# Sixteen counters in place of twelve for the transfers of a two-layer attention and MLP kernel

## The chip, the cores and the metric

The kernel runs on one core of a Trainium2 chip. A core has five engines with an instruction stream each: PE (matrix products), ACT (activation functions), DVE (elementwise work and reductions), POOL (elementwise work) and SP (which here only issues transfers). Each engine runs its own stream strictly in order; streams meet only through semaphores, which one instruction raises and another waits for. Transfers (DMAs) are issued by SP and, for two of them, by ACT; each raises its semaphore by 16 when it has landed. The metric is the device time of one execution in microseconds (us), and the number to predict is the median of several runs.

## The reference

Two layers, each of sliding-window attention and an MLP, both with a layer norm ahead and a residual behind, on one sequence of 2048 tokens of width 512:

```python
def _A_ref(x, wqkv, wo):                 # H = 32 heads, Dh = 16, window W = 256
    q, k, v = split(x @ wqkv)
    scores = einsum("bhqd,bhkd->bhqk", q, k) * (Dh ** -0.5)
    mask = (i - j >= 0) & (i - j < W)
    p = softmax(where(mask, scores, -1e9))
    return merge_heads(p @ v) @ wo

def _B_ref(x, w1, b1, w2, b2):           # F = 1792
    return gelu(x @ w1 + b1) @ w2 + b2

x = A_x
for _ in range(2):                       # the same weights both times
    x = x + _A_ref(layernorm(x), A_wqkv, A_wo)
    x = x + _B_ref(layernorm(x), B_w1, B_b1, B_w2, B_b2)
```

All inputs are bfloat16. B_x is not used.

## The kernel before

**Tiling.** The 2048 tokens are 16 tiles of 128 rows, held in SBUF as `X` for the whole program; two layers make 32 tile steps. A pair of tiles is an attention block (16 blocks, `attention`, line 894); the MLP takes two to four tiles at a time (`JOBS`, line 361; `mlp`, line 1080). For each tile `layernorm` (line 723) runs a chain: `bn_stats` and `bn_aggr` on DVE (lines 730 and 732), an addition of epsilon (line 734), a power on POOL (`rstd`, line 737), the scaling `xn` on DVE (line 740), and then a transposition, on PE (line 36 in the profile, by way of `_Slots.transpose`) with a copy out of PSUM (`evac`, line 714), or for later tiles through a scratch tensor in HBM by two transfers (`put` and `get`, lines 755 to 763). Projections to Q, K and V follow (`first_proj`, line 827, for the first block; `proj`, line 834), K by a product with a parity mask (lines 850 and 858), then the scores (line 928), the exponential on ACT (`E`, line 937), the mask (line 958), the product with V (line 1010), and the output projection. All matmuls go through `_Slots.matmul`, so the profile shows them as line 32.

**Order.** Each operation is a node. The list `ORDER` (line 413) fixes one global order of all nodes by hand, which fixes each engine's stream; `TURNS` and `BANKS` fix which engine takes an operation that has a choice, and the PSUM banks. `_List.run` (line 231) only works out planned start and end times for that order. Nothing of this depends on the number of counters.

**Waits.** `_Sched.op` (line 89) is called for each node in the global order. It works out what the node must wait for: the last writer of all that it reads, the last writer and the readers of all that it writes. A dictionary `know` holds what each engine is already sure of, from its own earlier waits and, through `snap`, from what the engine it waited for knew; a wait that is already covered is left out. For a transfer there is one wait more: transfers take the counters `dma0`, `dma1`, ... in turn, whoever issues them, and a transfer waits until the transfer before it on its counter has landed (lines 98 to 102):

```python
        if dma:
            counter = "dma%d" % (self.dma_rr % self.N_DMA_SEMS)
            self.dma_rr += 1
            inc = 16
            need(counter, self.cnt_val[counter])
```

`spread` (line 135) takes matmul operations that have more than one wait and puts the further ones at earlier matmuls, if the planned times allow it. `wait_all_dma` (line 131) makes SP wait for every counter at the end.

**The loads at the start.** There are fifteen, emitted in this order: 0 is tile 0 of X; 1 to 4 are quarters of the Q and K parts of Wqkv (Q first half, K first half, Q second half, K second half); 5 the V part; 6 the tiles 4 to 7 of X; 7 b1; 8 Wo; 9 the tiles 8 to 15 of X; 10 W1; 11 W2; 12 b2 (broadcast to 128 rows); all on SP. 13 is tile 1 of X and 14 the tiles 2 and 3, both issued by ACT, where they are the first instructions. The next transfer (15) comes at 114 us and belongs to the MLP's layer norm; in all there are 120, the last 17 of which write the output, mixed with the others.

```python
        load_x(0, 1, 2450.0)
        load_x(1, 1, 2650.0, "act")
        load_x(2, 2, 4500.0, "act")
```

**PE at the start.** `clear` (line 666) runs 13 matmuls on zeros (lines 675 and 676) ahead of all other PE work.

Of the kernel before, what the change touches and what calls it, by code (L numbers as in the profile page):

```python
# [55 lines left out]
class _Sched:  # L56

    ENGINES = ("pe", "act", "dve", "pool", "sp")
    N_DMA_SEMS = 12
    LOOK = 96  # L60
    COUNTERS = ("pe", "act", "dve", "pool") + tuple("dma%d" % i for i in range(N_DMA_SEMS))

# [26 lines left out]
    def op(self, eng, fn, reads=(), writes=(), inc=1, dma=False, start=0.0, end=0.0, n=1, joins=(), behind=None):  # L89
# [8 lines left out]
# [3 lines that stand above are left out]
# [1099 lines left out]
```

## Time and profile before

| | |
|---|---|
| device time, median of 3 runs | 460.27 us (459.19 to 461.04) |
| device time of the profiled execution | 463.4 us |
| its span, first to last instruction | 461.5 us |
| mean granted PE clock | 0.985 |
| PE busy | 438.4 us, 95% |
| ACT busy | 387.4 us, 84% |
| DVE busy | 369.4 us, 80% |
| POOL busy | 239.4 us, 52% |

The profile's page gives busy time by engine, the span in 40 equal slices (a digit is tenths), and the chain of work that ended last: followed back from the last instruction, at each step to what released it. Further views of the trace give that chain in order of time, a timeline of merged instructions (start, length, engine, line, operation, written and read tiles; in brackets the idle time of the engine before it and what ended it), sums by stretch of time with the granted PE clock, and for transfers the time from issue to landing. A letter q behind an engine's name (SPq, ACTq) is its sequencer, which issues transfers and waits. PEld is PE's loading of weights, which overlaps the matmuls.

### The profile page before, as it was taken

How to read it: one execution, taken by the hardware profiler on the slowest of the kernel's cores; microseconds unless marked ns; L12 is line 12 of the kernel's file. 1: busy time of each engine (PE TensorE's matmuls, PEld its weight loads, DVE VectorE, ACT ScalarE, POOL GpSimd, SP SyncE). 2: the span in 40 equal slices, each digit the busy share in tenths (PEclk: the TensorE clock that was granted, in tenths of full speed). 3: DMA queues.
4: the chain of work that ended last, by engine and by line, in shares of the span. 5: the costliest groups of instructions: out<-in, count | busy, mean ns of one | idle time of the engine just before them, and what ended most of it. 6: DMA issues, size and time to landing. Idle time of an engine off the chain costs nothing.

```text
span 461.5 us, 19292 instructions
## 1 busy us (share of the span) xinstructions
PE 438.4 (95%) x8764; PEld 233.9 (51%) x8764; DVE 369.4 (80%) x723; ACT 387.4 (84%) x462; POOL 239.4 (52%) x297
## 2 busy tenths in 40 slices
PE   4898999898998999999999999999999999999997
PEld 1755563554453454554444545445464453445665
DVE  1899988889995799997988789998999877777602
ACT  1399999999996998897998899989988899784262
POOL 2357466662756445663588726575534515291230
PEclk8699999999998999999999999999999999999999
DMA  8920000000150031521031011222312202012101
GB/s 255 371 71 4 5 3 1 4 2 9 40 98 3 13 38 41 98 40 26 24 83 26 13 26 37 72 42 33 59 37 62 37 24 68 7 50 60 57 1 45
DMA packets 74462, 22.87 MB, mean 50 GB/s; under 512 B 61324, under 2 KB 73868, under 8 KB 74380
## 3 DMA queue, kind: packets, MB, share of 16 engines
q1 hardware_dynamic: 73964, 21.24, 19.8%
q8 instruction: 68, 1.11, 1.0%
q10 hardware_dynamic: 416, 0.39, 0.3%
q14 instruction: 14, 0.11, 0.1%
HBM read 13.77 MB, written 7.86 MB: 47 GB/s over the span
## 4 chain that ended last, share of the span: by engine, by line
PE 77%; ACT 14%; DVE 3%; DMA 3%; issue 1%; SPq 0%
PE ps L32 77%; ACT E L937 12%; DMA X<-in_A_x_dram 1%; DMA scr_x<-xs_ 1%; DVE KT L858 1%; DMA Wqkv_sb<-in_A_wqkv_dram 1%; ACT gT L1103 1%; PE ps L36 1%; DVE stat L730 0%; DVE xs_ L750 0%; DVE X L795 0%; ACT gT L1095 0%; ACT L937 0%; ACT L1103 0%; DVE TT L1023 0%
## 5 line engine op out<-in xcount | busy, mean ns | idle before, releaser
L937 ACT ACTIVATE E<-ps 128x1024 bf16<-128x1024 f32 x304 | 285.9, 1045 | 24.1 <-PE ps L32 22.8
L958 POOL TENSOR_TENSOR E<-E,mask 128x512 bf16<-128x512 bf16 (+1 forms) x128 | 134.3, 1063 | 91.8 <-DVE E L958 33.3
L32 PE MATMUL ps<-W_sb,gT 128*128 128x512 bf16 (+1 forms) x462 | 119.8, 374 | 0.9 <-issue 0.6
L32 PE MATMUL ps<-xnTB,W_sb 128*128 128x512 bf16 (+1 forms) x560 | 116.5, 339 | 1.1 <-ACT E L937 0.5
L32 PE MATMUL ps<-xnTA,Wqkv_sb 128*128 128x256 bf16 (+1 forms) x544 | 75.6, 273 | 2.0 <-ACT E L937 1.2
L32 PEld LDWEIGHTS ps<-xnTB,W_sb 128*128 128x128 bf16 x560 | 51.3, 98 | 46.0 <-ACT E L937 5.1
L1103 ACT ACTIVATE gT<-ps,b1T 128x512 bf16<-128x512 f32 (+1 forms) x92 | 48.4, 589 | 25.1 <-PE ps L32 24.7
L795 DVE TENSOR_TENSOR X<-X,ps 128x512 bf16<-128x512 bf16 x63 | 42.6, 678 | 32.3 <-PE ps L32 31.8
L32 PE MATMUL ps<-QT,KT 32*64 32x320 bf16 (+4 forms) x2976 | 65.5, 259 | 2.8 <-ACT E L937 1.2
L32 PEld LDWEIGHTS ps<-W_sb,gT 128*128 128x128 bf16 x462 | 41.0, 98 | 44.5 <-issue 8.1
L32 PEld LDWEIGHTS ps<-xnTA,Wqkv_sb 128*128 128x128 bf16 x544 | 48.9, 101 | 24.5 <-ACT E L937 4.3
L958 DVE TENSOR_TENSOR E<-E,mask 128x512 bf16<-128x512 bf16 (+1 forms) x134 | 52.8, 421 | 3.6 <-ACT E L937 3.3
L32 PEld LDWEIGHTS ps<-QT,KT 32*64 32x64 bf16 x2976 | 27.8, 103 | 49.5 <-ACT E L937 32.5
L32 PE MATMUL ps<-E,Va 64*17 64x128 bf16 (+3 forms) x3872 | 46.5, 229 | 5.5 <-issue 3.0
L730 DVE BATCH_NORM_STATS2 stat<-X 128x6 f32<-128x512 bf16 x64 | 43.2, 680 | 9.5 <-DMA X<-in_A_x_dram 9.1
L1023 DVE STREAM_TRANSPOSE TT<-ps 128x1024 f32<-128x1024 f32 x32 | 39.9, 1247 | 13.1 <-PE ps L32 12.8
L737 POOL TENSOR_TENSOR rstd<-veps,mhalf 128x1 f32<-128x1 f32 x64 | 37.2, 586 | 24.3 <-DVE veps L734 22.5
L32 PEld LDWEIGHTS ps<-E,Va 64*17 64x17 bf16 x3872 | 36.7, 85 | 22.5 <-PE ps L32 8.2
L1028 POOL TENSOR_TENSOR TM<-TT,Rc 128x512 bf16<-128x512 f32 x21 | 22.2, 1058 | 43.9 <-DVE Rc L1026 31.4
L1067 POOL TENSOR_TENSOR X<-X,b2b 128x512 bf16<-128x512 bf16 x32 | 36.7, 1156 | 12.0 <-DVE E L958 6.5
L858 DVE TENSOR_TENSOR KT<-ps,parmask 128x1024 bf16<-128x1024 f32 x30 | 36.3, 1209 | 4.9 <-PE ps L32 4.8
L32 PE MATMUL ps<-Wqkv_sb,xnTA 128*128 128x512 bf16 x128 | 37.6, 386 | 0.4 <-issue 0.3
(52 smaller groups left out, 343.0 us busy)
## 6 DMA issues: line engine op xcount, KB each, us to landing
scr_x<-xs_ SPq DMA_DIRECT2D x44, 128.0 KB, 2.0
W_sb<-in_B_w_dram SPq DMA_DIRECT2D x2, 1792.0 KB, 15.2
xnTB<-scr_x SPq DMA_DIRECT2D x26, 128.0 KB, 2.7
xnTA<-scr_x SPq DMA_DIRECT2D x18, 128.0 KB, 3.7
out_dram<-X SPq DMA_DIRECT2D x15, 128.0 KB, 1.8
Wqkv_sb<-in_A_wqkv_dram SPq DMA_DIRECT2D x4, 256.0 KB, 4.1
X<-in_A_x_dram SPq DMA_DIRECT2D x1, 1024.0 KB, 10.7
Wqkv_sb<-in_A_wqkv_dram SPq DMA_DIRECT2D x1, 512.0 KB, 6.3
```

The source lines that it names most:

```text
L32: return self.e.matmul(*a, **k)
L36: return self.e.transpose(*a, **k)
L730: add("dve", lambda e, B: e.bn_stats(stat6[:, k6, :], X[:, t, :]), 590, reads=["X%d" % t], writes=["st%d" % k6], prio=prio)
L737: add("pool", lambda e, B: e.tensor_tensor(out=rstd[:, k : k + 1], in0=veps[:, k : k + 1], in1=mhalf[:], op=ALU.pow), 535, reads=["ve%d" % ...
L795: add("dve", lambda e, B: e.tensor_tensor(out=X[:, t, :], in0=X[:, t, :], in1=ps[:, B[g][0], :], op=ALU.add), d_psum(512), reads=["X%d" % ...
L858: add("dve", lambda e, B, g=g, i=i: e.tensor_tensor(out=KT[:, kb, :, 2 * i : 2 * i + 2, :].rearrange("p a c q -> p a (c q)"), in0=ps[:, B[ ...
L937: add("act", lambda e, B, g_=g_, gi=gi: e.activation(E[:, 2 * gi : 2 * gi + 2, e0 : e0 + 512], ps[:, B[g_][0] : B[g_][0] + 2, :], AF.Exp, ...
L958: op = lambda e, B, Ew=Ew, Mw=Mw: e.tensor_tensor(out=Ew, in0=Ew, in1=Mw, op=ALU.mult)
L1023: add("dve", lambda e, B: e.transpose(TT[:, s].rearrange("p a c q d -> p a (c q d)"), ps[:, B[g][0] : B[g][0] + 2, :].rearrange("p a n -> ...
L1028: mul = lambda e, B: e.tensor_tensor(out=TM[:, sm].rearrange("p c q a d -> p a (c q) d"), in0=TT[:, s, :, :, :, 0:Dh].rearrange("p a c q d ...
L1067: add("pool", lambda e, B: e.tensor_tensor(out=X[:, t, :], in0=X[:, t, :], in1=b2b[:], op=ALU.add), 1110, reads=["X%d" % t, "b2b"], writes ...
L1103: add("act", lambda e, B, g=g, fc=fc: e.activation(gT[:, fc, 0:M], ps[:, B[g][0], 0:M], AF.Gelu_apprx_tanh, bias=b1T[:, fc : fc + 1], scal ...
```

## The change

The number of counters for transfers goes from 12 to 16. With it the tuple `COUNTERS`, the semaphores taken, the turn in which transfers take them, and the waits at the end follow.

```diff
@@ -56,7 +56,7 @@
 class _Sched:
 
     ENGINES = ("pe", "act", "dve", "pool", "sp")
-    N_DMA_SEMS = 12
+    N_DMA_SEMS = 16
     LOOK = 96
     COUNTERS = ("pe", "act", "dve", "pool") + tuple("dma%d" % i for i in range(N_DMA_SEMS))
```

Transfer number k takes counter k mod 16 in place of k mod 12, and waits for number k - 16 in place of k - 12. Order, engines and PSUM banks stay as they are.

## The prediction

> **What bounds the kernel now.** I read the page's head and its clock row first, then the first stretch of the chain of waits, then the timelines of ACT, DVE and PE there, and last the windows that cover the hand-over to the long middle part.
>
> ```profile
> span 461.5 us, 19292 instructions
> ...
> PEclk8699999999998999999999999999999999999999
> ```
>
> The span is 461.5 us of a profiled execution of 463.4 us, so 1.9 us lie around it. The clock row is lowest in the first two slices (11.5 us each). So the start is unlike the rest, and the chain of waits says why:
>
> ```profile
> 1.22 3.14 DMA Wqkv_sb<-in_A_wqkv_dram
> 4.37 0.02 issue
> 4.39 6.76 DMA X<-in_A_x_dram
> ...
> 13.30 0.61 ACT xnTA L718
> 13.90 0.05 issue
> 13.95 0.61 PE ps L32 x4
> ```
>
> The chain goes from a weight load that lands at 1.22 + 3.14 = 4.36 us straight into the load of an X tile, which waits for no weight. That is a borrowed wait: tile 1 of X (128 rows) needs nothing from Wqkv. The timelines of ACT, DVE, POOL and PE give the rest:
>
> ```profile
> 4.39 1.35 ACTq L689 DMA_DIRECT2D X<-in_A_x_dram  x2
> ```
> ```profile
> 2.84 0.69 DVE L730 BATCH_NORM_STATS2 stat<-X 128x6 f32<-128x512 bf16 x1 [1.66 <-DMA X<-in_A_x_dram]
> 3.57 0.18 DVE L732 BATCH_NORM_AGGREGATE statmv<-stat 128x2 f32<-128x6 f32 x1
> 11.18 0.69 DVE L730 BATCH_NORM_STATS2 stat<-X 128x6 f32<-128x512 bf16 x1 [7.42 <-DMA X<-in_A_x_dram]
> ...
> 12.12 0.15 DVE L734 TENSOR_SCALAR veps<-statmv 128x1 f32<-128x1 f32 x1
> 12.19 0.41 DVE L740 TENSOR_SCALAR xn<-X,statmv,rstd 128x512 bf16<-128x512 bf16 x1
> ...
> 18.01 0.42 DVE L716 COPY xnTA<-ps 128x512 bf16<-128x512 bf16 x1 [1.36 <-PE ps L36]
> ...
> 18.86 1.29 DVE L850 TENSOR_TENSOR KT<-ps,parmask 128x512 bf16<-128x512 f32 x2
> ```
> ```profile
> 1.24 4.91 PE L32 MATMUL ps<-gT 128*128 128x512 bf16 x13 [1.24 <-DVE gT L664]
> 12.65 0.61 PE L36 MATMUL ps<-ident,xn 128*128 128x128 bf16 x4 [6.51 <-DVE xn L740]
> ...
> 20.67 0.42 PE L32 MATMUL ps<-QT,KT 32*64 32x256 bf16 x16
> ```
>
> ACT issues its two X loads (tile 1, then tiles 2 and 3) only at 4.39. DVE works in order: it has tile 0's statistics at 3.57 + 0.18 = 3.75, then stands 7.42 us before tile 1's, and tile 0's own normalisation (xn, 12.19) is queued behind them. PE ends its clearing matmuls at 1.24 + 4.91 = 6.15 and stands 6.5 us. The first scores come at 20.67. What follows is bound by ACT:
>
> ```profile
> 21.23:61.00 39.77, 36.90 (x859) 21.36 (x857) 38.14 (x82) 39.71 (x46) 24.09 (x30) 1.00 0.13 39
> ```
>
> The columns are the stretch, its length, then the busy time of PE, PE's weight loads, DVE, ACT and POOL, the granted clock, the DMA share and GB/s. From its first exponential (21.23) ACT is busy 39.71 of 39.77 us. A stage without a gap moves as a whole: what the start gains, its end gains.
>
> **The change, part by part.** Transfers take counters in turn, in emission order, and each waits for the last transfer on its counter. Fifteen early loads are emitted: thirteen on SP (numbers 0 to 12), then ACT's two (13 and 14). With 12 counters, 12, 13 and 14 fall on counters 0, 1 and 2, which belong to tile 0 of X, the first Wqkv piece and the second. That fits the trace: ACT's first issue comes 0.03 us after the first Wqkv piece landed. With 16, none of the fifteen shares.
>
> *Removed:* ACT's two waits. SP's own borrowed wait (b2b on tile 0, landed by 2.84) is over long before b2b's turn, so worth nothing. When does tile 1 land now? These are the issues, with KB each and us to landing:
>
> ```profile
> X<-in_A_x_dram SPq DMA_DIRECT2D x1, 512.0 KB, 7.9
> ...
> X<-in_A_x_dram SPq DMA_DIRECT2D x1, 128.0 KB, 2.0
> X<-in_A_x_dram ACTq DMA_DIRECT2D x1, 128.0 KB, 6.8
> ```
>
> The same 128 KB took 2.0 us into empty queues and 6.8 us into queues that SP had already filled. ACT's issue should come when the other engines start, about 0.85 us (tile 0's load was issued at 2.84 - 2.0 = 0.8, and ACT has nothing ahead of its own). So tile 1 lands between 2.9 and 7.6 us. I take 3.4: at 0.85 only tile 0 and a first piece of Wqkv are ahead, and 128 KB more at the 258 GB/s of that stretch (next fence) add 0.5 us. The Trainium skill (DMA: Bandwidth & Descriptors, section Queues, rings and completion order) says that each DMA engine takes turns between the queues it has work for, a packet at a time. By that rule ACT's load would share from its issue on, and land near 3.4 at any hour; the trace disagrees for a load that comes late, with its 6.8 us.
>
> *First term, to the first transpose.* DVE: tile 1's statistics from 3.77 take 0.69 + 0.18 + 0.15 and xn 0.41, with their gaps to about 5.3 us. That is before PE is free at 6.15. So the first transposes move from 12.65 to 6.15: **6.5 us**. The cover is the 0.85 us that DVE has over PE; tile 1 may land as late as 4.6 at no cost.
>
> *Second term, the clock.* Rows of the windows view, columns as above:
>
> ```profile
> 1.76:5.17 3.41, 3.41 (x10) 1.20 (x9) 0.88 (x2) 0.00 (x0) 2.43 (x10) 1.00 0.94 258
> 5.17:8.59 3.42, 0.97 (x5) 0.23 (x3) 0.00 (x0) 1.28 (x1) 0.00 (x0) 1.00 0.96 299
> ...
> 12.00:15.41 3.41, 2.07 (x18) 1.81 (x19) 3.29 (x12) 0.60 (x1) 2.01 (x5) 0.50 1.10 353
> 15.41:18.83 3.42, 3.42 (x35) 3.42 (x33) 2.06 (x4) 0.87 (x2) 1.09 (x2) 0.50 1.04 402
> ...
> 104.16:107.57 3.41, 2.41 (x140) 1.37 (x116) 3.26 (x9) 3.41 (x5) 1.15 (x1) 1.00 0.02 5
> ...
> 138.29:141.71 3.42, 1.33 (x78) 0.74 (x56) 0.45 (x1) 0.63 (x2) 1.15 (x1) 1.00 0.00 0
> 141.71:145.12 3.41, 3.41 (x24) 0.97 (x23) 2.08 (x4) 2.32 (x3) 1.86 (x2) 0.50 0.02 5
> ```
>
> A stretch of 3.4 us with PE busy 0.97 or 1.33 us is followed by half the clock; one with 2.41 keeps it. After the change the idle time between the clearing matmuls and the projections is only ACT's copy of the first transposed tile, 0.61 plus hand-over, some 0.75 us, so PE is busy about 2.65 of 3.41: the full clock stays. Now the projections run at half clock from 12.65 to 18.83. Of this the continuous part, 13.95 to 18.83, is 4.88 us, which becomes 2.44; the transposes at 12.65 save another 0.2. Together 2.6 at most, the lower end is nothing. DVE caps it: from xn's end (12.60) to the end of the second K product (18.86 + 1.29 = 20.15) it needs 7.55 us, 1.36 of them waiting for PE; 6.19 after 5.3 makes 11.5, as late as PE's own 6.15 + 8.02 - 2.6 = 11.5. The scores then start near 11.65 where they started at 20.67, which is 9.0 in all. **Second term: 2.5 us.**
>
> *Moved, and its price.* ACT's 384 KB now go ahead of the Wqkv pieces, and delay them by 0.39 MB at 299 GB/s, 1.3 us. SP's issues of these pieces, and how long they took to land:
>
> ```profile
> 1.22 2.61 SPq L694 DMA_DIRECT2D Wqkv_sb<-in_A_wqkv_dram  x5
> 3.88 0.51 SPq L689 DMA_DIRECT2D X<-in_A_x_dram  x1
> ```
> ```profile
> DMA to landing us min/median/max: 3.1/4.6/6.3
> ```
>
> The piece that is needed first is the second of five, issued at 1.22 + 2.61/5 = 1.74 if the five are even, and landing 3.1 to 4.6 us behind; with 1.3 added it is there by 7.6 at the latest, against a use near 7.3: 0 to 0.3 us. The bytes up to tiles 4 to 7 stay the same: they land at 3.88 + 7.9 = 11.8, and DVE wants them behind the K product, 11.5: 0.3 us, on DVE and not at the end of the chain there. PE's program code also arrives by DMA; these are the stretches 20 to 28 and 28 to 35 us:
>
> ```profile
> DMA  9999999999999999999999997544221000000000
> ...
> q8 instruction: 1, 0.02, 0.8%
> ```
> ```profile
> GB/s 0 0 0 0 0 0 0 94 0 0 0 0 0 0 47 0 0 0 0 0 0 0 0 0 0 0 0 0 0 0 0 0 0 0 0 0 0 0 0 0
> ```
>
> One code block of 16 KB came between 24 and 28 (none shows from 16 to 24), the next at 28 + 7 x 0.175 = 29.2, and the loads are drained at 20 + 32 x 0.2 = 26.4. After the change the code is wanted 9 us sooner, in the midst of the loads. For all of this I take **0.5 us**, between 0 and the price in the third rival.
>
> *Added:* four more waits at SP's end, and about two on PE, which ACT's waits used to cover (weights landed). Rows of such waits are 17 to 28 ns:
>
> ```profile
> L177 SPq EVENT_SEMAPHORE  x14: 17/17/28, 133.5 to 461.0; - x14
> ```
>
> Six make 0.1 to 0.2 us: nothing. Behind the early loads the DMAs are spread over 350 us; the twelfth before is landed long since, and I found no wait of SP on it that binds.
>
> Sum: 6.5 + 2.5 - 0.5 = **8.5 us**. On the profiled execution 463.4 becomes 454.9. The three runs have a median 3.1 us lower, 460.27, and the same gain makes **451.8 us**.
>
> **The rivals.** *Half clock stays* through the projections, because the clearing matmuls and the grid of 3.4 us fall otherwise: only 6.5 of the gain, 453.8. Against it: 2.41 of 3.41 us was enough at 104 us. *Tile 1 still takes 6.8 us*, because SP's loads go first whatever the hour: it lands at 7.6 in place of 11.15, PE idles past 8.6 and loses the clock as before, gain 3.5, 456.8. Against it: at 0.85 us SP has filled almost nothing. *The code waits for the loads.* PE wants the first block by the time the second came, 29.2; less 9.0 that is 20.2. If it comes only when the loads are drained, 26.4, PE stands 6.2 us and 9.0 - 6.2 - 0.3 = 2.5 is left, 457.8, right at what can be told from no change, and counted there. *Nothing is left:* a later wait for something fixed in time swallows it, 460.3; against it stands ACT without a gap from 21.23 to 61, and loads that end at 26.4. *Slower:* PE's code blocks miss its pace at other places. One such place is in the trace:
>
> ```profile
> 140.59 0.56 PE L32 MATMUL ps<-E,Va 64*17 64x256 bf16 x38 [2.09 <-issue]
> ```
>
> PE stands 2.09 us without a wait the profile can name, and the next 3.41 us run at half clock, 1.7 more: 3.8 us. A few added instructions and another phase could make new ones; three cancel the gain, four make 460.3 - 8.5 + 15.2 = 467.0. Nothing suggests that moving the whole program creates four.
>
> **How the numbers follow.** Chances: my forecast (gain 7 to 10.5) 0.67, half clock 0.13, tile 1 late 0.08, code 0.05, nothing 0.03, slower 0.04. Likeliest 451.8; its own range is 449.8 to 453.5. The range 449.3 to 456.9 takes in the half clock and the late tile. A measurement here can tell about 0.5%, 2.3 us, from no change (the three runs lie within 1.85). Faster than 457.97: 0.67 + 0.13 + 0.08 = 0.88; within: 0.05 + 0.03 = 0.08; slower 0.04.
>
> **What would show it.** In the changed profile: ACT's two issues near 0.9 us; tile 1's statistics within 0.5 us of 3.8; the first transposes near 6.2; no half clock after 8.6; the first exponential near 12.2 and ACT without a gap from there for 40 us. A first exponential at 12.2 with an end less than 7 us earlier would prove the carrying-over wrong; PE standing for "issue" near 19 us would speak for the code; half clock up to 12 or beyond for the first rival.

## The result and the profile after

The changed kernel has a median of 454.52 us over 4 runs (452.74 to 455.6), beside 460.49 us for the kernel before in the same session (459.19 to 461.04). The ratio is 0.987, 95% interval 0.983 to 0.991. That is 6.0 us less, and faster by more than the 0.5% that can be told. Two repetitions, each beside runs of the kernel before on the same chip, are among the experiments: 0.986 (0.982 to 0.989) and 0.988 (0.984 to 0.993). One run of the kernel before in the first of them, 466.0 us, was a slow one and is left out of what is compared. The profiled execution after took 455.6 us; its head and clock row on the page:

```profile
span 453.9 us, 19297 instructions
...
PEclk9999999999989999999999999999999999999999
```

The low clock of the first two slices is gone (the record of the clock begins only at 5.91 us here; the last section takes that up). One slice, the twelfth (125 to 136 us), has an 8.

The chain of waits of the changed kernel at its start (start, length, what):

```profile
0.79 2.79 DMA X<-in_A_x_dram
3.57 0.02 issue
3.60 0.70 DVE stat L730
...
8.73 1.15 DVE xn L740
9.88 0.05 issue
9.93 0.40 PE ps L36 x4
10.33 2.25 PE ps L32 x32
12.58 0.02 issue
12.60 0.66 ACT QT L718 x2
13.26 9.17 ACT E L937 x10
```

No weight load stands in it any more. The chain begins with tile 0 of X, then runs on DVE, statistics and normalisations, from 3.60 to 9.88, and only then comes PE. Timelines of ACT, DVE, POOL and PE in the same stretch, cut to the rows that answer the prediction:

```profile
0.78 0.91 ACTq L689 DMA_DIRECT2D X<-in_A_x_dram  x2
...
13.14 3.78 ACT L937 ACTIVATE E<-ps 128x1024 bf16<-128x1024 f32 x4
```
```profile
3.60 0.69 DVE L730 BATCH_NORM_STATS2 stat<-X 128x6 f32<-128x512 bf16 x1 [2.42 <-DMA X<-in_A_x_dram]
...
4.42 0.66 DVE L730 BATCH_NORM_STATS2 stat<-X 128x6 f32<-128x512 bf16 x1
...
5.51 0.41 DVE L740 TENSOR_SCALAR xn<-X,statmv,rstd 128x512 bf16<-128x512 bf16 x1
...
8.65 1.22 DVE L740 TENSOR_SCALAR xn<-X,statmv,rstd 128x512 bf16<-128x512 bf16 x1
...
11.04 1.28 DVE L850 TENSOR_TENSOR KT<-ps,parmask 128x512 bf16<-128x512 f32 x2
```
```profile
8.81 0.92 POOL L662 MEMSET Va<- 128x192 bf16 x1
```
```profile
1.24 5.27 PE L32 MATMUL ps<-gT 128*128 128x512 bf16 x13 [1.24 <-DVE gT L664]
6.35 0.39 PE L36 MATMUL ps<-ident,xn 128*128 128x128 bf16 x4
...
9.93 0.40 PE L36 MATMUL ps<-ident,xn 128*128 128x128 bf16 x4 [0.55 <-DVE xn L740]
...
12.58 0.42 PE L32 MATMUL ps<-QT,KT 32*64 32x256 bf16 x16
```

ACT issues its loads at 0.78 in place of 4.39. DVE goes from tile 0's statistics straight into tile 1's; the hole of 7.42 us is closed. The first transposes come at 6.35 (12.65 before), the first scores at 12.58 (20.67), the first exponential at 13.14 (21.23): **8.1 us sooner**. What was not foreseen stands in the first DVE row: tile 0 itself is late (3.57 us in place of 2.82).

The windows view of the changed kernel (stretch, length, busy time of PE, PEld, DVE, ACT and POOL, granted clock, DMA share, GB/s):

```profile
5.91:9.32 3.41, 2.72 (x39) 2.20 (x37) 3.33 (x11) 0.72 (x2) 2.24 (x6) 1.00 1.12 323
9.32:12.74 3.42, 2.86 (x54) 2.51 (x52) 2.93 (x6) 1.49 (x4) 0.41 (x1) 1.00 1.10 349
13.14:53.14 40.00, 36.97 (x861) 21.45 (x860) 38.67 (x82) 39.94 (x46) 24.06 (x30) 1.00 0.33 113
...
128.70:132.11 3.41, 1.67 (x97) 0.85 (x96) 1.33 (x2) 2.06 (x3) 2.20 (x2) 1.00 0.39 38
132.11:135.53 3.42, 3.21 (x59) 1.57 (x60) 1.88 (x3) 1.64 (x2) 0.24 (x1) 0.51 0.02 5
```

The projections keep the full clock, with PE busy 2.72 us of 3.41. ACT is busy 39.94 of 40.00 us from its first exponential, so the lead is carried over. The last two rows are the 8 of the clock row: a stretch with PE busy 1.67 us, and half the clock behind it. They belong to a stand of 1.8 us that the experiments take up.

### The profile page after: what moved, and what is told of

Same layout as the page of the kernel before. It is cut to its first block, busy times and chain, and to the rows that moved or that the text cites. A ratio compares the mean times of both kernels' runs of the same rounds, so it can differ in the third digit from the quotient of the medians.

```text
span 453.9 us, 19297 instructions
## 1 busy us (share of the span) xinstructions
PE 436.0 (96%) x8764; PEld 232.0 (51%) x8764; DVE 369.3 (81%) x723; ACT 387.2 (85%) x462; POOL 239.1 (53%) x297
## 3 DMA queue, kind: packets, MB, share of 16 engines
q8 instruction: 69, 1.13, 1.0%
## 4 chain that ended last, share of the span: by engine, by line
PE 78%; ACT 15%; DVE 4%; DMA 1%; issue 1%
PE ps L32 77%; ACT E L937 13%; DVE stat L730 1%; DMA scr_x<-xs_ 1%; ACT gT L1103 1%; DVE xn L740 1%; DMA X<-in_A_x_dram 1%; DVE KT L858 0%; DVE xs_ L750 0%; DVE X L795 0%; ACT gT L1095 0%; PE ps L36 0%; ACT L937 0%; ACT L1103 0%; ACT QT L718 0%
## 5 line engine op out<-in xcount | busy, mean ns | idle before, releaser
L32 PE MATMUL ps<-xnTA,Wqkv_sb 128*128 128x256 bf16 (+1 forms) x544 | 74.0, 267 | 2.7 <-ACT E L937 1.4
L32 PEld LDWEIGHTS ps<-xnTA,Wqkv_sb 128*128 128x128 bf16 x544 | 47.2, 98 | 24.7 <-ACT E L937 4.6
L1023 DVE STREAM_TRANSPOSE TT<-ps 128x1024 f32<-128x1024 f32 x32 | 39.9, 1247 | 13.4 <-PE ps L32 13.2
```

The lines of the kernel that those rows point to most:

```text
L32: return self.e.matmul(*a, **k)
L1023: add("dve", lambda e, B: e.transpose(TT[:, s].rearrange("p a c q d -> p a (c q d)"), ps[:, B[g][0] : B[g][0] + 2, :].rearrange("p a n -> ...
```

## The experiments

Diffs are against the kernel before, unless the text says the changed kernel. "Issue" in a row of PE is a stand for which the profile has no wait to name.

**The pair again.** The profiled execution of before was some 3 us longer than its median, so both kernels were profiled once more, unchanged (before is `same12`, after `again16`).

> The kernel before once more, to see how much of its own profile repeats. Theory (the gain is made at the start, nothing else differs): ACT's first load goes out at 4.4 us, the first exponential starts between 20.9 and 21.6 us. Rival (part of the difference between the two profiled executions is the place near 138 us where PE stands 2.1 us and then loses the clock for 3.4 us): that stall is absent or of another size here, and the span is up to 3.8 us off 461.5 though the start is the same.

> Sixteen counters once more, to size the gain. By the traces the last exponential comes 7.95 us sooner and the last instruction 7.6 us; if that is the gain of every execution, the two medians here differ by 7 to 8 us (ratio 0.983 to 0.985). Rival: the gain in time is 6 us as in the first runs (ratio 0.987), the profiled execution of before having been a long one.

Sixteen counters: 453.41 us (6 runs) beside 460.76 (10 runs), ratio 0.986 (0.982 to 0.989): by the medians 7.4 us, in the 7 to 8 expected, by the ratio between that and the rival's 0.987. In `same12` ACT's first load goes out at 4.78, not at 4.4 as expected, and the first exponential still comes at 21.23. In `again16` it comes at 12.79, 8.4 us sooner. The spans, 458.5 and 451.7, lie only 6.8 apart, so 1.6 us are lost on the way. PE's timeline of `same12`, then of `again16`, then of the changed kernel's first profile, at one and the same product with V:

```profile
139.94 0.56 PE L32 MATMUL ps<-E,Va 64*17 64x256 bf16 x38 [0.98 <-issue]
```
```profile
131.98 0.56 PE L32 MATMUL ps<-E,Va 64*17 64x256 bf16 x38 [1.78 <-issue]
```
```profile
132.32 0.91 PE L32 MATMUL ps<-E,Va 64*17 64x256 bf16 x38 [1.81 <-issue]
```

This is the place that the prediction priced at 2.09 + 1.7 us in the kernel before. It stands 0.98 in one execution of the kernel before and 2.09 in the other; with sixteen counters 1.78 and 1.81. Half the clock follows in one execution of each kernel (behind 2.09 and 1.81) and in the other not. Length alone doesn't decide it: `vaearly16` below stands 2.09 us there and keeps the clock, as its stand falls into two of the 3.4 us stretches, with PE busy 2.11 and 2.32 us. So one place moves a single execution by up to some 3 us (1.1 us of standing and the prediction's 1.7 for the clock), with or without the change. Two profiles that differ there are not to be subtracted: 461.5 - 453.9 = 7.6 has the half clock on both sides, 458.5 - 451.7 = 6.8 on neither. A second such place, longer with sixteen counters, in the changed kernel and in `again16`:

```profile
207.56 0.45 PE L32 MATMUL ps<-E,Va 64*17 64x256 bf16 x26 [0.68 <-issue]
```
```profile
205.45 0.45 PE L32 MATMUL ps<-E,Va 64*17 64x256 bf16 x26 [0.69 <-issue]
```

At that product PE stood 0.40 in the first profile of before and did not stand in `same12`. Against `same12`, the two places lose 0.80 + 0.69 = 1.5 us, about what the spans miss. Compared matmul by matmul, `again16` leads `same12` by 8.8 us ahead of the first place, by 8.0 behind it and by 6.9 behind the second.

**Is it the counters or the borrowed wait?** Twelve counters, but ACT's loads (19 and 20 in the hand-written order) are emitted directly behind tile 0 (18), as numbers 1 and 2, so that no counter of theirs has been used:

```diff
-            4, 5, 15, 16, 17, 18, 21, 22, 23, 24, 25, 26, 27, 28, 29, 30, 8, 9, 10, 11, 12, 31, 32, 6, 19, 35, 36,
-            0, 1, 3, 20, 2, 37, 38, 42, 43, 44, 39, 90, 45, 46, 40, 41, 61, 91, 47, 83, 84, 85, 92, 93, 94, 7, 48,
+            4, 5, 15, 16, 17, 18, 19, 20, 21, 22, 23, 24, 25, 26, 27, 28, 29, 30, 8, 9, 10, 11, 12, 31, 32, 6, 35, 36,
+            0, 1, 3, 2, 37, 38, 42, 43, 44, 39, 90, 45, 46, 40, 41, 61, 91, 47, 83, 84, 85, 92, 93, 94, 7, 48,
```

> Twelve counters, with ACT's two loads emitted as numbers 1 and 2, so that they fall on free counters; W1, W2 and b2 take over the shared ones. Theory (all of the gain is ACT's borrowed wait): the same as sixteen counters, first exponential at 13.1 us within 0.3, 453 to 455 us. Rival (more counters help elsewhere too, behind the loads): the first exponential at 13.1 but over 2 us of the gain missing, 456.5 or more.

454.19 us (4 runs), ratio 0.986 (0.981 to 0.991), the same as sixteen counters. ACT's timeline of this kernel:

```profile
0.78 0.90 ACTq L689 DMA_DIRECT2D X<-in_A_x_dram  x2
```

First exponential at 13.02, span 452.2. The whole gain is the early issue of two loads; four more counters as such do nothing for the time that these runs could tell.

**Which of the two loads?** With 13 counters, number 13 (tile 1) waits for tile 0 and number 14 (tiles 2 and 3) for the first Wqkv piece; with 14, tile 1 waits for nothing and tiles 2 and 3 for tile 0. The diff of `n13`; `n14` has 14 there:

```diff
-    N_DMA_SEMS = 12
+    N_DMA_SEMS = 13
```

> Thirteen counters: tile 1 now shares with tile 0 of X, tiles 2 and 3 with the first Wqkv piece. Tile 1 is issued about 2.9 us, tiles 2 and 3 at 4.4 as with twelve. Theory (what counts is how much of SP's queue is ahead of a load when it is issued): tile 1 lands 5 to 7 us behind its issue, at 8 to 10, tiles 2 and 3 near 12 as before, and since DVE takes tile 3's statistics ahead of tile 1's normalisation, the first exponential comes at 20 to 21 us: under 1 us gained, 460. Rival (only tile 1 counts): first exponential at 18 to 19.

> Fourteen counters: tile 1 waits for nothing, tiles 2 and 3 for tile 0 of X, so they are issued near 3.2 us. Theory: tile 1 at 3.3, first transposes near 6.3 as with sixteen; tiles 2 and 3 land 5 to 7.3 us behind their issue, at 8.5 to 10.5, DVE stands for them, PE stands and loses its clock, first exponential at 16.5 to 19.3 us: a quarter to a half of the gain, 456 to 459. Rival (only tile 1 counts): first exponential near 13, all of the gain.

One run each, 457.36 and 458.07 us, beside 459.55 for the kernel before: in sign as expected, too close to rank. The first exponentials tell more: 19.02 with 13 (20 to 21 expected; what came is the upper end of the rival's 18 to 19), 17.54 with 14 (16.5 to 19.3). The chain of waits with 14:

```profile
0.79 2.75 DMA X<-in_A_x_dram
3.54 0.02 issue
3.56 6.65 DMA X<-in_A_x_dram
10.20 0.02 issue
10.23 0.69 DVE stat L730
```

With tile 1 free, the first transposes are early (5.94), and then PE stands 3.87 us for tile 2's normalisation and loses the clock until 14.1. So the notion that only tile 1 counts falls: half of the 8 us hangs on tiles 2 and 3. DVE's timeline with 13:

```profile
7.55 0.69 DVE L730 BATCH_NORM_STATS2 stat<-X 128x6 f32<-128x512 bf16 x1 [3.75 <-DMA X<-in_A_x_dram]
...
11.72 0.69 DVE L730 BATCH_NORM_STATS2 stat<-X 128x6 f32<-128x512 bf16 x1 [2.75 <-DMA X<-in_A_x_dram]
```

Tile 1, issued at 2.88, landed at 7.53: 4.65 us. For the same 128 KB the issues at 0.78, 2.88 and 4.39 thus give 2.7 to 3.0, 4.65 and 6.76 us (6.2 to 6.8 in all the profiles with an issue at 4.1 to 4.8). The landing time grows with the time of issue, and so with what SP has queued by then. The Trainium skill (DMA: Bandwidth & Descriptors, section Queues, rings and completion order) has each DMA engine take turns between its queues; by that alone the time of issue should matter little, and in these runs it matters, as in the first row of 6.8 us.

**The clock term by itself.** Leave the borrowed wait, and keep PE at work with 28 more clearing matmuls until tile 1 lands:

```diff
-                    r = e.matmul(ps[:, b, :], gT[:, 0, 0:P], zero, start=True, stop=True)
+                    r = e.matmul(ps[:, b % 8, :], gT[:, 0, 0:P], zero, start=True, stop=True)
...
-        for n, took in ((8, 3420.0), (5, 1500.0)):
+        for n, took in ((8, 3420.0), (33, 1500.0)):
```

> Twelve counters with the borrowed wait kept, but 28 more clearing matmuls, so that PE is busy until about 12.2 us and keeps its full clock while tile 1 is late. It measures the second term of the prediction by itself. Theory: first transposes at 12.6 to 12.8, full clock from there, first exponential near 19.4 (1.8 us sooner than 21.23, which is what the traces show between first transpose and first scores), 458.5 us. Rival (the projections are held by DVE's chain and not by PE's clock): first exponential within 0.4 us of 21.2, no change of time.

The first exponential came at 19.52, 1.7 us sooner than in `same12`, as expected. But not all of that is the clock: tile 1 also landed 0.9 us sooner (10.35 beside 11.23), so the transposes started at 11.85 in place of 12.73, and only 0.8 us was gained from there to the scores. And the time rose to 474.67 us (4 runs), ratio 1.030 (1.025 to 1.036). PE's waits of `same12`, then of this kernel (what it waited for, us in total, times, longest):

```profile
PE ps L32 <- issue: 8.3, 44, 1.0
```
```profile
PE ps L32 <- issue: 20.3, 54, 1.8
```

Twelve more microseconds in which PE stands for nothing that can be named, spread over the program. (Both traces lack 77 matmul records, and show some 40 short stands that a trace with all records doesn't: the first profile of before has 3.9 us in 5. Stands over 0.3 us alone are 2 of 1.5 us in `same12`, 4 of 3.6 us in the first profile of before and 12 of 13.7 us here.) Two things could be at fault: the waits of later matmuls (the planned times differ) or the place of the program's code blocks, which now lie 56 PE instructions (28 pairs of weight load and matmul) later. The page of the changed kernel counts the transfers of code (queue, packets, MB, share):

```profile
q8 instruction: 69, 1.13, 1.0%
```

1.13 MB in 69 packets makes 16.4 KB a packet; if these are PE's, its 8764 matmuls and 8764 weight loads are 254 to a packet, so about 256 instructions of 64 B fill one. The next two kernels leave every later wait where it was, and add only PE instructions at the start: 56 in the one, 256, a whole block, in the other.

```diff
-                for b in range(n):
-                    r = e.matmul(ps[:, b, :], gT[:, 0, 0:P], zero, start=True, stop=True)
+                for b, w in [(b, 512) for b in range(n)] + [(b % 8, 64) for b in range(28 * (n == 5 and not isinstance(e, _Count)))]:
+                    r = e.matmul(ps[:, b, 0:w], gT[:, 0, 0:P], zero[:, 0:w], start=True, stop=True)
```

(`_Count` only counts instructions for the plan, which so stays as it was. In `phase256` 128 matmuls of 112 columns in place of 28 of 64.)

> Twelve counters, 28 more clearing matmuls of 64 columns each (under 1 us, in time in which PE stands anyway; the clock is lost as before), all later waits in their places. It asks why the longer clearing cost 14 us in the earlier run although its first exponential came 1.7 us sooner. Theory (PE's code comes in blocks, and 28 more matmuls with their weight loads shift every later block border by 56 instructions, to places where PE is fast): first exponential at 21.2 as before, new stretches of over 0.7 us in which PE stands for no wait that the profile names, 469 to 477 us. Rival (the clock or the waits placed elsewhere did it): 461 us, no new stretches.

> Twelve counters, 128 more clearing matmuls of 112 columns each: 256 instructions, a whole block if a block holds 256, so that the borders fall where they fell before; and PE is busy until about 12.2 us, so that the clock stays full. It measures the second term of the prediction without the shift of borders. Theory: first exponential at 19.5 and about 1.7 us gained at the end, 459.0 to 459.5. Rival (longer clearing is harmful whatever its length): 465 or more. Rival for the second term: first exponential at 21.2.

56 instructions: 472.62 us in one run, beside 462.32. 256 instructions: 460.61 us (10 runs), ratio 0.997 (0.994 to 0.999). PE's waits with 56, then with 256:

```profile
PE ps L32 <- issue: 19.8, 52, 1.9
```
```profile
PE ps L32 <- issue: 9.7, 45, 2.1
```

(With 256, 77 records are missing as well; stands over 0.3 us are 12 of 13.4 us with 56 and 3 of 3.0 us with 256.) A shift of the code by a part of a block costs 10 us; a shift by a whole block costs nothing, although it adds more instructions. Later waits stand alike in both, so what hurts is where the block borders fall against PE's fast passages.

The traces show the cause itself. Code comes on queue q8 in packets of 16,384 bytes, and in the fourteen profiles each of PE's 37 stands over 0.6 us "for issue" ends 1.2 to 1.6 us after such a packet has landed: PE stands for its code. The longest stand with 56 instructions ends 1.3 us behind a packet that landed at 304.41:

```profile
305.70 0.42 PE L32 MATMUL ps<-QT,KT 32*64 32x320 bf16 x15 [1.93 <-issue]
```

With 256 instructions the stand of `same12` behind 2748 recorded matmuls is found again behind 2876, at the same product, just the 128 added matmuls later. With 56 there is none over 0.3 us at that product. The Trainium skill (Runtime: NRT & Kernel Launch, section Instruction fetch mechanics) states that code is refilled in blocks of 16 KiB, 256 instructions, and that crossing a border is mostly hidden. The block size agrees with these two runs. The hiding holds at most borders (12 stands over 0.3 us beside 69 packets with 56 instructions) and fails at the others, with single stands of up to 2.1 us.

`phase256` is also the clean measure of the clock: PE is at work until 12.28, the first transposes start at 13.04, and to the first scores (19.72) it takes 6.68 us, where the kernel before took 20.67 - 12.65 = 8.02. **The full clock alone is worth 1.3 us there**, not the 2.5 that were forecast, and PE stands 0.74 us in that stretch for DVE's fourth normalisation. The time is 1.7 us less than the 462.32 beside it, as expected, though the first exponential came at 20.28 and not at 19.5, only 0.95 us sooner than in `same12`; tile 1 landed 0.3 us later than there (11.54).

**Can the new path be shortened?** Two places, both on the changed kernel. In `sp16` SP issues tile 1 and tiles 2 and 3 itself, right behind tile 0, so that they don't share the engines with tile 0. In `vaearly16` POOL's clearing of Va goes earlier in the order, out of the way of DVE's fourth normalisation, which takes 1.22 us beside it. First `sp16`, whose order is changed as in `ord12` too, then `vaearly16`:

```diff
-        load_x(1, 1, 2650.0, "act")
-        load_x(2, 2, 4500.0, "act")
+        load_x(1, 1, 2650.0)
+        load_x(2, 2, 4500.0)
```
```diff
-            0, 1, 3, 20, 2, 37, 38, 42, 43, 44, 39, 90, 45, 46, 40, 41, 61, 91, 47, 83, 84, 85, 92, 93, 94, 7, 48,
-            64, 86, 52, 49, 55, 87, 95, 96, 50, 88, 89, 53, 65, 62, 51, 97, 98, 13, 54, 99, 100, 58, 14, 59, 56,
+            0, 1, 3, 20, 2, 14, 37, 38, 42, 43, 44, 39, 90, 45, 46, 40, 41, 61, 91, 47, 83, 84, 85, 92, 93, 94, 7, 48,
+            64, 86, 52, 49, 55, 87, 95, 96, 50, 88, 89, 53, 65, 62, 51, 97, 98, 13, 54, 99, 100, 58, 59, 56,
```

> Sixteen counters, but tile 1 and tiles 2 and 3 are issued by SP as its second and third loads, behind tile 0 in one queue, in place of ACT's queue beside it. It tests the step that fell short: tile 0 landed at 3.57 us in place of 2.82. Theory (the two queues share the engines, so tile 0 pays for tile 1, and DVE's chain starts that much later): tile 0 at 2.8, tile 1 by 3.5, first exponential 0.4 to 0.8 us sooner than 13.1 (12.3 to 12.7). Rival (Wqkv, now two issues later, takes tile 0's place as the bound): first exponential at 13.0 or later, PE waiting for a transfer.

> Sixteen counters, and POOL's memset of Va (0.92 us) moved from 8.8 us, where DVE's fourth normalisation took 1.22 in place of 0.41 us beside it, to about 3.7 us. Theory (DVE's chain sets the first exponential, and this contention is on it): the normalisation takes 0.4 us, first exponential 0.5 to 0.8 us sooner than 13.1, some 0.6 us less at the end. Rival (PE's chain is right behind): under 0.2 us.

`sp16`: 453.46 us (5 runs), ratio 0.983 (0.981 to 0.985). Tile 0 landed at 2.91 as meant, but the first exponential came at 13.09, not at the 12.3 to 12.7 expected. The chain of waits shows what was late next:

```profile
1.24 5.73 PE ps L32 x13
6.97 0.44 PE ps L36 x4
```

The clearing matmuls, the same thirteen, lasted until 6.97 and now set the start; for a transfer, as the rival had it, PE does not wait. `vaearly16`: 454.14 us (5 runs), ratio 0.982 (0.979 to 0.984). Rows of DVE and ACT:

```profile
8.55 0.40 DVE L740 TENSOR_SCALAR xn<-X,statmv,rstd 128x512 bf16<-128x512 bf16 x1
```
```profile
12.23 2.87 ACT L937 ACTIVATE E<-ps 128x1024 bf16<-128x1024 f32 x3
```

The fourth normalisation is back at 0.40, and the first exponential comes 0.6 to 0.9 us before that of the changed kernel. Both at once, beside the changed kernel unaltered:

> Sixteen counters beside the version below on the same chip. Theory: 7 to 8 us less than before, ratio 0.983 to 0.985, first exponential at 12.7 to 13.2. Rival: 6 us or less, 0.987 and up.

> Sixteen counters with both changes at the start: tile 1 and tiles 2 and 3 behind tile 0 in SP's queue, and the memset of Va early. Theory (with tile 0 at 2.9 and the normalisation at 0.4 us DVE has slack, and PE's clearing and its clock set the first exponential): 11.8 to 12.6 us, according to when the full clock comes, 0.5 to 1 us sooner than sixteen counters alone; in time 0.1 to 0.2% below the run beside it, which five rounds may not tell apart. Rival (what is gained at the start is lost behind it): the same time as the run beside it or more, though the first exponential is sooner.

453.57 us (6 runs, ratio 0.988, 0.984 to 0.993) for the changed kernel, 453.59 us (6 runs, 0.986, 0.984 to 0.989) with both. Beside 459.55 for the kernel before, the changed kernel gains 6.0 us here: the rival's 6 us or less, not the 7 to 8 expected. `spva16` has its first exponential at 12.86 (11.8 to 12.6 expected), `again16b` at 13.17. Tenths of a microsecond at the start don't show in the whole, and no version was shown to beat sixteen counters alone.

## Why the prediction held, and where it was off

The forecast was 451.8 us with a gain of 8.5; measured are 454.5 (6.0 us) and in the repetitions 453.4 and 453.6 (7.4 and 6.0). The mechanism was right, but the time alone doesn't show it: it fits the 453.8 of the rival with half the clock better than the forecast, and only the windows rows tell the two apart. The start gave 8.1 to 8.4 of the 9.0 us forecast, and more than the 0.5 us allowed for was lost behind it. The time lies inside the range (449.3 to 456.9), 1.6 to 2.7 us above the forecast, at or up to 1.0 us above the upper end of the likeliest case's own range (453.5).

- *What is removed.* Right: the chain lost the weight load, ACT's loads left at 0.78. `ord12` shows that this alone is the change.
- *Tile 1 at 3.4, statistics within 0.5 us of 3.8.* Tile 1 was in time (3.77 here, 3.46 in `again16`), but its statistics started at 4.42. The step "DVE: tile 1's statistics from 3.77" failed, by taking tile 0's landing as unmoved. Tile 0 landed at 3.57 here and 3.22 in `again16` (2.82 before), because ACT's loads now share the engines with it: in `n14`, with tile 1 alone beside it, it landed at 3.54, in `sp16`, where they are queued behind it, at 2.91. The delay goes through to the first exponential, which comes 9.57 to 9.58 us behind tile 0's landing in the changed kernel, `again16`, `again16b` and `ord12`. The bound was worked out for the moved transfer and not for those beside it.
- *First term, 6.5 us.* Measured 12.65 - 6.35 = 6.3. The cover of DVE over PE (0.85 us) took up tile 0's delay, as it was there for. The 0.2 us short are the clearing matmuls, 5.27 us in place of 4.91. "PE is free at 6.15" was read from one execution; in `again16` they took 4.58 us, and the transposes started at 5.66.
- *Second term, 2.5 us.* The mechanism was right: no half clock after 8.6, PE busy 2.72 of 3.41 (2.65 forecast). The size was off. Transposes to scores took 12.58 - 6.35 = 6.23 us, 1.8 less than before (1.4 less in `again16`, whose transposes start sooner). The cap by DVE was named with the right length, 6.19 us; it ran from 5.92 to 12.32, 6.40 us, but its start had been put at 5.3. PE's projections, held 0.55 us by DVE's fourth normalisation, ended at 12.58, not at 11.5. So 0.6 of the 0.9 us by which the scores missed 11.65 is tile 0's delay. That is worked out from the rows; the run with tile 0 in time, `sp16`, had another bound, the clearing.
- *Carrying over.* Right: ACT without a gap for 40 us. At the end of the span 6.5 to 7.6 us of the 8.1 to 8.4 were left. In `again16` (6.8) and `again16b` (6.5) that is less than the 7 us which the prediction set as its sign, for a first exponential at 12.2. What is missing there is lost further on, the next point.
- *0.5 us for code and late loads.* Mis-sized, and put in the wrong place. Nothing was lost near 19 us. What was lost, 0.5 to 1.6 us by spans, fits the stands at two products with V, near 132 and 206 us.
- *Rivals.* "Half clock stays" and "tile 1 late" did not come: 2.72 of 3.41 us, 3.77 us. `n14` shows what the latter is like when it happens to tiles 2 and 3. "The code waits for the loads" did not come: the first code packet on q8 landed at 17.5 us, and PE's first stand for issue over 0.3 us is at 82. "Slower", by code blocks that miss PE's pace, didn't come either, yet its mechanism is real: `warm12` and `phase56` show it at 10 to 14 us. The prediction gave 4% to it on the ground that moving the program in time makes no new places; what makes them is moving the program in its code, which this change hardly does: the place near 132 us lies behind 2764 matmuls before and after.

What stays open: why the stands near 132 and 206 us differ between executions of one kernel. Both ends move: in the two profiles of before, the code for the first place landed at 139.24 and 138.59, and PE was ready for it at 138.50 and 138.97, which makes 2.09 and 0.98 us. That the change lengthens the first place is not shown (0.98 to 2.09 us in the two profiles of before and in `phase256`, 1.54 to 1.81 in three of the changed kernel). The second place is longer in all three of the changed kernel (0.68 to 0.69 us, beside 0.40 at most). But `ord12`, with the same early loads, has no stand over 0.3 us there, and neither have `sp16`, `vaearly16` and `spva16`, with as many counters; so neither the early loads nor the counters make it by themselves.

## What to carry to other kernels

When a load waits for something it doesn't need, look at how counters are shared: two loads emitted earlier were worth as much here as four more counters. When a transfer is freed, work out the landing of its neighbours too, above all of the one that the first engine is waiting for. Before a few instructions are added to an engine that streams thousands, test a second version that adds a whole code block: if the two differ, the time went into block borders and not into the work.

## What the runs showed of the hardware that was not expected

- Adding 56 instructions to PE's stream of some 17,500 (8764 matmuls and as many weight loads) raised the time by 10 us, 256 by nothing. PE's stands "for issue" of over 0.3 us went from 1.5 us to 13.4, and with 256 were 3.0. Each long one ended 1.2 to 1.6 us after 16,384 bytes of code had landed.
- The thirteen clearing matmuls took 4.35 us in `vaearly16`, 5.27 in the changed kernel and 5.73 in `sp16`. PE starts at its slower rate: they follow each other 0.43 us apart at first and 0.22 us apart from 4.05, 5.91 and, in `sp16`, only behind the last of them, from 7.26. These are the times at which the record of the clock begins; ahead of its first entry the windows view shows 1.00 (as in the prediction's row from 1.76 to 5.17), and PE still runs at half pace. The Trainium skill (TensorE: Matmul & The Clock Gate, Part 1: The HAM clock gate) states that the window on which the clock is judged runs freely and does not reset with the kernel; that the pace rises at another time in each execution agrees with it. In `sp16` the longest of them took away what tile 0's earlier landing should have brought.
- A normalisation of 128x512 on DVE took 1.22 us in place of 0.41 while POOL cleared Va (0.92 us), and 0.40 when that was moved away. The kernel before has the same row (1.22 us at 15.42), hidden there behind PE at half clock.
